# Stage 1 of a fused attention and expert kernel: score matmuls placed one by one, and the mixed tile moved to the front of its pair, with three products

## The chip, the cores and the metric

The kernel runs on one core of a Trainium2 chip. The time is that of one execution on the device in microseconds (us). Beside the runs that give the time, one execution is recorded by the hardware profiler, and all rows below are of that one.

## The reference

Three layers follow one another. The first is attention with pooled queries, the second a mixture of four small attention experts of which each token uses two, the third a gated layer with a causal convolution over five tokens. The change is in the first, which in the reference is:

```python
# q, k, v: 4 batches x 8 heads x 1152 x 64, float32
q_pool = q.reshape(B, H, S // 2, 2, D).mean(axis=3)          # 576 queries of a head
scores = scale * np.matmul(q_pool, k.transpose(0, 1, 3, 2))   # 576 x 1152
scores = scores - np.max(scores, axis=-1, keepdims=True)
attn = np.exp(scores)
attn = attn / (np.sum(attn, axis=-1, keepdims=True) + 1e-09)
out = np.matmul(attn, v)
```

## The kernel before

Stage 1 is this attention. It works through 16 pairs of heads, one after the other. A head has 576 queries, four blocks of 128 and a rest of 64, so a pair has nine score tiles of 128 queries by 1152 keys: four of each head, and one that holds the last 64 queries of both heads (called the mixed tile below). A tile goes through these steps:

- `scores` (L405): the tile's 1152 columns in three groups of 384, each in a PSUM bank of its own. Two score tiles fit in PSUM (pool `ps_s`, six banks).
- `rowmin` (L418, L421): VectorE reduces the tile to a row minimum `nm`. The scores carry a minus sign, so this is the maximum.
- `expo` (L423, L427): ScalarE takes the exponential from PSUM into `p` in SBUF and adds up the row.
- `transp` (L456, L464): TensorE transposes `p` in nine 128x128 pieces, three to a PSUM bank. One such three is called a T group here. Two banks serve all T groups (pool `ps_t`, tile `t`), and ScalarE (L472) or VectorE (L474) copies each group out into `pt`. The string table `EVAC` says which engine takes which group: one string for a tile of the pair, one letter for a group, D for VectorE and A for ScalarE.
- `av` (L476, L494), called a burst here: once per half of a pair (a unit), 18 matmuls multiply the transposed weights with the values. Before them the row sums' reciprocals are spread by transposes (L453), and after them VectorE multiplies the result by these (L496, `xf`). The burst's result lies in a bank of `ps_t` too.

Scores are made with split numbers. A float32 operand is cut into a high and a low part, each in the type `fp32r`. For a head's own tiles the 128 contraction rows hold the 64 dimensions twice: the high part of the queries above the low part (`qst`), against the same part of the keys in both halves (`ka` and `kb`, one for each head). Two matmuls, one for the keys' high part and one for the low, so give all four products. In the mixed tile the queries of head 0 stand beside zeros, and those of head 1 too, so that the two heads' results land on different rows; that takes two matmuls for each head, four for a group of columns.

The split itself is made for the next pair while one is worked on (`prep`, L359): GpSimd writes the high and low parts of queries and keys into `hlq` and `hlk`, and SyncE's DMAs copy them into `qst`, `ka` and `kb` (L377, L381 to L383).

The order of all this is written out by hand. `ORDER` (L399) is a string that is run through once per pair. S puts a group's score matmuls next (two, or four for the mixed tile), T a T group, X an exponential, H the reciprocals of a unit's sums, A a burst. The row minimum follows a tile's last S by itself (`score`, L621). `head` is called at the first S of each tile and carries GpSimd's and SyncE's work along. `UNITS` (L401) lists a pair's tiles: four in the first unit, and five in the second, of which the mixed tile (2, 4) is last. In pairs 1 to 9 VectorE also turns the third layer's weights into float32 during each burst (`decode`, L86 to L105).

TensorE takes its instructions in the order in which they were written, and so do the others. The engines wait for one another by semaphores.

Of the kernel before, what the change touches and what calls it, by code (L numbers as in the profile page):

```python
# [20 lines left out]
def tile_kernel(ctx, tc, q, k, v, w_gate, wq, wk, wv, wo, w_val, conv_w, w_out, wo_t, out):  # L21
    nc = tc.nc
# [294 lines left out]
    with ExitStack() as s1:  # L317
# [13 lines left out]
        for par in range(2):  # L331
            pair = [qpool.tile([P, 4 * P + 2 * R64], F32R, name=f"qst{par}{h}") for h in range(2)]
            act.activation(pair[0][:, 4 * P + R64:], zero, AF.Copy)
            act.activation(pair[1][:, 4 * P:4 * P + R64], zero, AF.Copy)
            qst.append(pair)
# [23 lines left out]
        def prep(n):  # L359
# [6 lines left out]
            data[n] = [qst[n % 2], kst, vn]  # L366
# [12 lines left out]
            def qmove():  # L379
                for r in range(2):  # L380
                    nc.sync.dma_start(f(qa[64 * r:64 * r + 64, 0:SQ]), f(hlq[0:64, r, :]))  # L381
                    nc.sync.dma_start(f(qb[64 * r:64 * r + 64, 0:512]), f(hlq[64:128, r, 0:512]))
                    nc.sync.dma_start(f(qb[64 * r:64 * r + 64, 512 + R64:]), f(hlq[64:128, r, 512:]))  # L383

            def qgroup():
                pool.tensor_scalar(qp, qp, -scale / 2, None, op0=ALU.mult)
                pool.tensor_copy(hlq[:, 0], qp)
                late.append(lambda: pool.tensor_tensor(out=hlq[:, 1], in0=qp, in1=f(hlq[:, 0]), op=ALU.subtract))
                late.append(qmove)
# [9 lines left out]
        ORDER = "TSTSSTTXSTTSSHTTXSTTSSTTXSSSASTSSTXSTTSSTTXSTTSSHTTXSTTSSTTSTXSSA"  # L399
        EVAC = ('DDA', 'ADD', 'AAD', 'DAA', 'DAD', 'DAA', 'DDA', 'ADD', 'AAA')  # L400
        UNITS = ([(0, 0), (0, 1), (1, 0), (1, 1)], [(0, 2), (0, 3), (1, 2), (1, 3), (2, 4)])  # L401
        tiles = [(n, u, i, ht) for n in range(len(pairs)) for u in range(2) for i, ht in enumerate(UNITS[u])]
        soft, pts, rss = {}, {}, {}

        def scores(m, g):  # L405
            n, u, i, (h, t) = tiles[m]
            qs, ks, vn = data[n]
            if g == 0:
                soft[m] = dict(s=ps_s.tile([P, G, 512], F32, name="s"))
            ps = soft[m]["s"][:, g, :]  # L410
            if h < 2:
                ops = [(qs[h][:, t * P:(t + 1) * P], ks[h][:, s, g * GW:(g + 1) * GW]) for s in range(2)]
# [10 lines left out]
        def expo(m):  # L423
            d = soft[m]
            n, u, i, _ = tiles[m]
# [3 lines left out]
        def shares(m):  # L429
# [3 lines left out]
            if i == k - 1:  # L433
# [6 lines left out]
                def copies():  # L440
                    eng = pool if n or u else dve
                    eng.tensor_copy(rm[:, 0:2].rearrange("p t (h d) -> p t h d", d=D), both)  # L442
                    if u == 1:
                        pool.tensor_copy(rm[:, 2], rs[:, 4:5].to_broadcast([P, P]))
# [3 lines left out]
        def spread_shares(n, u):  # L448
# [3 lines left out]
            for t in range(2 + u):  # L452
# [3 lines left out]
        def transp(m, g):  # L456
            n, u, i, (h, t) = tiles[m]
            p = soft[m]["p"]
            if i == 0 and g == 0:
                pts[n, u] = pt_p.tile([P, C, 2, 256 + R64 * u], F32, name=f"pt{u}")  # L460
# [15 lines left out]
        def av(n, u, between):  # L476
# [4 lines left out]
            N = 256 + R64 * u  # L481
# [5 lines left out]
            if u:  # L487
# [10 lines left out]
            def low():  # L498
                pool.tensor_tensor(out=xt[:, 1, :], in0=x, in1=f(xt[:, 0, :]), op=ALU.subtract)
                late.append(lambda: nc.sync.dma_start(f(x_d[b][:, hp, :, 256 * u:256 * u + N]), f(xt)))  # L500
# [9 lines left out]
        def first():  # L510

            b, hp = pairs[0]
            bufs = pt_p.tile([P, C, 2, 256 + R64], F32, name="pt1").rearrange("p c h q -> p (c h q)")
# [4 lines left out]
            data[0] = [qst[0], kst, vn]  # L518
# [10 lines left out]

            def qhigh(h, i):  # L530
                a, z = cuts[i]
                pool.tensor_scalar(qst[0][h][:, a + (R64 if h and i == 2 else 0):z + (R64 if h and i == 2 else 0)], qd[h][:, 0, a:z], -scale / 2, None, op0=ALU.mult)

            def qpart(h, i):
                a, z = cuts[i]
                o = R64 if h and i == 2 else 0
                qp = qd[h][:, 0]
                if i == 0:
                    act.activation(qst[0][h][:, a + o:z + o], qp[:, a:z], AF.Copy, scale=-scale / 2)
# [595 lines left out]
```

## Time and profile before

| what | value |
|---|---|
| time, median of three runs | 780.28 us (778.89 to 780.52) |
| the profiled execution's own time | 779.28 us |
| its span, first to last instruction | 777.5 us |
| TensorE busy | 756.8 us, 97% of the span |
| VectorE, ScalarE, GpSimd busy | 571.9, 447.9 and 306.5 us |
| stage 1, up to the last burst's start | 502.60 us |

The span is the stretch from the first instruction to the last. The profiled execution took 1.8 us more than its span, and 1.0 us less than the median. A matmul's recorded duration includes its way through the array, so that durations of neighbours overlap; what a matmul costs in a row of others is read from the distance between starts. A row with "x6" merges six neighbours of one kind: its first number is the start of the first one.

### The profile page before, as it was taken

What the parts mean: (1) busy time and instruction counts of PE and PEld (TensorE: products, weight loads), DVE (VectorE), ACT (ScalarE), POOL (GpSimd) and SP (SyncE); (2) the same over time, 40 slices, a digit from 0 to 9 for tenths busy, and PEclk for the clock granted to TensorE, in tenths of its full rate; (3) what the DMA queues carried; (4) which work ended last, traced back from release to release, by engine and by line L of the source; (5) the groups of instructions that cost most, each with busy time, mean ns of one, the idle gap of its engine ahead of it and who ended that gap; (6) DMA issues with size and microseconds to landing.
All of it is one profiled execution on the core that took longest, in us unless ns stands there. A gap on an engine that the chain in (4) does not pass through costs nothing.

```text
span 777.5 us, 14803 instructions
## 1 busy us (share of the span) xinstructions
PE 756.8 (97%) x5332; PEld 621.9 (80%) x5332; DVE 571.9 (74%) x1063; ACT 447.9 (58%) x988; POOL 306.5 (39%) x412
## 2 busy tenths in 40 slices
PE   6999999999999999999999999999999999989998
PEld 4777878778778778778787787888989889868887
DVE  5777888888988888756766675447679798888730
ACT  5566566466556656665664665425564554648632
POOL 4564574764765754743534511023222222220000
PEclk9999999999999999999999999999999999999999
DMA  7777867878789689668458483375545563900212
GB/s 237 184 194 222 246 180 232 230 202 248 186 240 265 171 242 266 158 199 244 111 171 230 123 258 123 90 205 112 167 108 123 134 186 93 293 1 14 81 57 94
DMA packets 86825, 134.51 MB, mean 173 GB/s; under 512 B 21600, under 2 KB 58976, under 8 KB 86752
## 3 DMA queue, kind: packets, MB, share of 16 engines
q1 hardware_dynamic: 86752, 133.57, 61.2%
q8 instruction: 42, 0.69, 0.4%
q14 instruction: 31, 0.25, 0.1%
HBM read 53.37 MB, written 21.76 MB: 97 GB/s over the span
## 4 chain that ended last, share of the span: by engine, by line
PE 86%; DVE 7%; ACT 3%; issue 1%; SPq 1%; DMA 1%; POOL 1%; POOLq 0%; DVEq 0%; ACTq 0%
PE s L416 21%; PE t L464 20%; PE t L494 18%; PE a L242 7%; PE o L1051 6%; PE a L275 4%; PE a L850 3%; PE s L750 2%; PE a L715 2%; DVE gp L215 2%; PE a L822 1%; PE t L453 1%; SPq L524 1%; ACT p L771 1%; DVE nm L760 1%
## 5 line engine op out<-in xcount | busy, mean ns | idle before, releaser
L421 DVE TENSOR_REDUCE nm<-s 128x1 f32<-128x1152 f32 x144 | 195.4, 1357 | 37.3 <-PE s L416 30.9
L427 ACT ACTIVATE p<-s,nm 128x1152 f32<-128x1152 f32 x144 | 175.9, 1222 | 37.0 <-DVE nm L421 28.3
L464 PE MATMUL t<-ident,p 128*128 128x128 f32 x1296 | 194.2, 280 | 2.5 <-DVE pt L474 1.9
L472 ACT ACTIVATE pt<-t 128x384 f32<-128x384 f32 x224 | 99.9, 489 | 146.1 <-PE t L464 136.7
L464 PEld LDWEIGHTS t<-ident,p 128*128 128x128 f32 x1296 | 147.0, 141 | 41.4 <-ACT pt L472 17.1
L494 PE MATMUL t<-pt,vn 128*64 128x320 f32 (+1 forms) x1152 | 146.8, 408 | 0.0
L416 PE MATMUL s<-ka,qst 128*128 128x384 f32 x480 | 127.9, 370 | 6.8 <-ACT ka L545 6.8
L494 PEld LDWEIGHTS t<-pt,vn 128*64 128x64 f32 x1152 | 80.0, 137 | 55.8 <-issue 5.3
L416 PE MATMUL s<-kb,qst 128*128 128x384 f32 x480 | 120.8, 360 | 1.0 <-ACT p L427 0.9
L474 DVE COPY pt<-t 128x384 f32<-128x384 f32 x208 | 107.3, 548 | 13.1 <-PE t L464 10.0
L416 PEld LDWEIGHTS s<-kb,qst 128*128 128x128 f32 x480 | 79.7, 191 | 8.3 <-issue 6.2
L416 PEld LDWEIGHTS s<-ka,qst 128*128 128x128 f32 x480 | 78.2, 193 | 8.2 <-ACT ka L545 7.2
L786 POOL TENSOR_TENSOR p<-p,sm 128x512 f32<-128x512 f32 (+3 forms) x32 | 40.1, 1253 | 110.2 <-DVE sm L784 81.9
L442 POOL COPY rm<-rs 128x256 f32<-128x256 f32 x31 | 12.4, 400 | 130.4 <-DVE rs L437 122.5
L496 DVE TENSOR_TENSOR xf<-t,rb 128x256 f32<-128x256 f32 (+1 forms) x32 | 14.7, 458 | 63.2 <-PE t L494 62.3
L771 ACT ACTIVATE p<-s,nm 128x256 f32<-128x256 f32 (+3 forms) x64 | 33.1, 524 | 22.7 <-DVE nm L760 22.6
L371 POOL TENSOR_TENSOR hlk<-kt,hlk 128x384 fp32r<-128x384 f32 x45 | 45.2, 1005 | 1.0
L242 PE MATMUL a<-xh,wqk 128*128 128x288 f32 x288 | 43.0, 299 | 2.1 <-DVE pt L800 2.1
L215 DVE SCALAR_TENSOR_TENSOR gp<-x,cw,gp 128x572 f32<-128x572 f32 (+3 forms) x48 | 40.7, 849 | 2.6 <-ACT gp L871 2.1
L503 POOL CAST xt<-xf 128x256 fp32r<-128x256 f32 (+1 forms) x32 | 13.6, 424 | 72.6 <-DVE xf L496 72.5
L242 PEld LDWEIGHTS a<-xh,wqk 128*128 128x128 f32 x288 | 39.4, 188 | 3.1 <-DVE pt L800 2.5
L760 DVE TENSOR_REDUCE nm<-s 128x2 f32<-128x512 f32 (+4 forms) x40 | 32.4, 811 | 1.4
(176 smaller groups left out, 1091.9 us busy)
## 6 DMA issues: line engine op xcount, KB each, us to landing
ka<-hlk SPq DMA_DIRECT2D x90, 192.0 KB, 3.2
kb<-hlk SPq DMA_DIRECT2D x90, 192.0 KB, 3.6
vn<-in_v_dram SPq DMA_DIRECT2D x16, 576.0 KB, 7.8
k<-hl SPq DMA_DIRECT2D x32, 288.0 KB, 4.9
qt<-in_q_dram SPq DMA_DIRECT2D x15, 576.0 KB, 5.3
kt<-in_k_dram SPq DMA_DIRECT2D x15, 576.0 KB, 6.3
xh<-x_d SPq DMA_DIRECT2D x12, 576.0 KB, 6.2
x_d<-xt SPq DMA_DIRECT2D x16, 320.0 KB, 4.0
```

What stands on the lines that cost most here:

```text
L215: dve.scalar_tensor_tensor(out=gp[:, n:], in0=x[:, 0:SQ - n], scalar=cw[:, m, c:c + 1], in1=gp[:, n:], op0=ALU.mult, op1=ALU.add)
L242: pe.matmul(ps[:, 0:HQ], lhsT=wqk[wi][:, t, cs], rhs=xh[t][xi][:, qsl], start=o == 0, stop=o == len(ops) - 1)
L371: late.append(lambda: pool.tensor_tensor(out=hlk[:, 1, gs], in0=kt[:, gs], in1=f(hlk[:, 0, gs]), op=ALU.subtract))
L416: pe.matmul(ps[:, 0:GW], lhsT=a, rhs=c, start=o == 0, stop=o == len(ops) - 1)
L421: dve.tensor_reduce(d["nm"], d["s"][:, :, 0:GW], axis=AX.XY, op=ALU.min)
L427: act.activation(d["p"], d["s"][:, :, 0:GW], AF.Exp, bias=d["nm"], scale=-1.0, accum_out=sums[(2 * n + u) % len(sums)][:, i:i + 1])
L464: pe.transpose(ps[:, j * P:(j + 1) * P], p[:, g, j * P:(j + 1) * P], ident)
L472: act.activation(dst, src, AF.Copy)
L474: dve.tensor_copy(dst, src)
L494: pe.matmul(ps[64 * h:64 * h + 64, 0:N], lhsT=vn[:, h, j, :], rhs=pt[:, j, h, :], start=j == 0, stop=j == C - 1)
L771: act.activation(p[:, e * w:(e + 1) * w], ps[:, e, 0:w], AF.Exp, bias=nm[:, e:e + 1], scale=-1.0, accum_out=sm[:, e:e + 1])
L1051: pe.matmul(ps[:, 0:w], lhsT=hl[xi][:, kt, t * P - a:(t + 1) * P - a], rhs=end3["wo3"][:, kt, wi, c:c + w], start=o == 0, stop=o == len(op ...
```

## The change

The score matmuls are placed one by one. An S of the new `ORDER` is one matmul for a tile of a head, so that a T group can stand between the two matmuls of a group of columns. The row minimum gets a letter of its own, R, and the string is written anew.

The mixed tile becomes the first of its pair and of the first unit, which so has five tiles and the second four. The queries are reordered on the way in, so that the mixed tile holds queries 256 to 319. Its products are made in another way, except in pair 0: the operand `mixed` has the high and the low part of both heads' 64 queries as blocks on a diagonal, with zeros beside them, and it is multiplied with `hlk`, the split keys of both heads as GpSimd wrote them. High by high, low by high and high by low are three matmuls, in place of four; the product of the two low parts is not made. `mixed` is written by GpSimd in two copies. `qst` is 64 columns shorter, and two DMAs of a pair fall away. `EVAC` is written anew as well, with 13 D and 14 A as before.

```diff
-            data[n] = [qst[n % 2], kst, vn]
+            data[n] = [qst[n % 2], kst, vn, hlk]
...
-                    nc.sync.dma_start(f(qa[64 * r:64 * r + 64, 0:SQ]), f(hlq[0:64, r, :]))
-                    nc.sync.dma_start(f(qb[64 * r:64 * r + 64, 0:512]), f(hlq[64:128, r, 0:512]))
-                    nc.sync.dma_start(f(qb[64 * r:64 * r + 64, 512 + R64:]), f(hlq[64:128, r, 512:]))
+                    nc.sync.dma_start(f(qa[64 * r:64 * r + 64]), f(hlq[0:64, r, 0:4 * P]))
+                    nc.sync.dma_start(f(qb[64 * r:64 * r + 64]), f(hlq[64:128, r, 0:4 * P]))
+
+            def qlow():
+                pool.tensor_tensor(out=hlq[:, 1], in0=qp, in1=f(hlq[:, 0]), op=ALU.subtract)
+                for h in range(2):
+                    hs = slice(64 * h, 64 * h + 64)
+                    pool.tensor_copy(mixed[hs, :, hs], f(hlq[hs, :, 4 * P:]))
...
-        EVAC = ('DDA', 'ADD', 'AAD', 'DAA', 'DAD', 'DAA', 'DDA', 'ADD', 'AAA')
-        UNITS = ([(0, 0), (0, 1), (1, 0), (1, 1)], [(0, 2), (0, 3), (1, 2), (1, 3), (2, 4)])
+        EVAC = ('AAA', 'DDA', 'ADD', 'AAD', 'DAA', 'DDA', 'AAD', 'AAD', 'DDD')
+        UNITS = ([(2, 4), (0, 0), (0, 1), (1, 0), (1, 1)], [(0, 2), (0, 3), (1, 2), (1, 3)])
+        FIRST = ([(0, 0), (0, 1), (1, 0), (1, 1), (2, 4)], UNITS[1])
...
-                ops = [(qs[hh][:, 4 * P:], ks[hh][:, s, g * GW:(g + 1) * GW]) for hh in range(2) for s in range(2)]
-            for o, (a, c) in enumerate(ops):
-                pe.matmul(ps[:, 0:GW], lhsT=a, rhs=c, start=o == 0, stop=o == len(ops) - 1)
+                ops = [(last0[hh], ks[hh][:, s, gs]) for hh in range(2) for s in range(2)]
+            per = max(1, len(ops) // slots(m))
+            for c in range(o * per, min(len(ops), (o + 1) * per)):
+                pe.matmul(ps[:, 0:GW], lhsT=ops[c][0], rhs=ops[c][1], start=c == 0, stop=c == len(ops) - 1)
...
+            elif n:
+                ops = [(mixed[:, wi], kboth[:, xi, gs]) for wi, xi in THREE]
...
+                elif c == "R":
+                    if nr < M:
+                        rowmin(nr)
+                    nr += 1
```

The following rows show TensorE's program in the first unit of the second pair before the change: scores of one head's tiles (L416, `s<-ka` and `s<-kb`), T groups (L464, three transposes each), the spreading of the sums (L453), and the burst (L494).

```order
L464 MATMUL t<-ident,p 128x128 x6
L416 MATMUL s<-ka,qst_138 128x384 x2
L464 MATMUL t<-ident,p 128x128 x6
L416 MATMUL s<-ka,qst_138 128x384 x4
L464 MATMUL t<-ident,p 128x128 x6
L416 MATMUL s<-ka,qst_138 128x384 x2
L464 MATMUL t<-ident,p 128x128 x6
L416 MATMUL s<-ka,qst_138 128x384 x4
L464 MATMUL t<-ident,p 128x128 x6
L416 MATMUL s<-kb,qst_139 128x384 x6
L453 MATMUL t<-ident,rm 128x128 x2
```

And these show it after the change, from the mixed tile's matmuls of one pair (L433, `s<-hlk,mixed`) to the next tile's; L482 are the T groups.

```order
L433 MATMUL s<-hlk,mixed 128x384
L482 MATMUL t<-ident,p 128x128 x6
L433 MATMUL s<-hlk,mixed 128x384 x5
L482 MATMUL t<-ident,p 128x128 x3
L433 MATMUL s<-hlk,mixed 128x384 x3
L482 MATMUL t<-ident,p 128x128 x6
L433 MATMUL s<-ka,qst_134 128x384 x2
L482 MATMUL t<-ident,p 128x128 x3
L433 MATMUL s<-ka,qst_134 128x384
L482 MATMUL t<-ident,p 128x128 x3
L433 MATMUL s<-ka,qst_134 128x384 x2
L482 MATMUL t<-ident,p 128x128 x3
```

Two T groups in a row were parted by two or four score matmuls by turns. Now two in a row have at least three matmuls ahead of them in nearly every place, and many T groups stand alone, with one or two matmuls between.

The next rows are VectorE's program around the burst of a pair's first unit (256 columns) in the stretch in which it decodes weights, before the change: copies of T groups (L474), two row minima (L421), the seven decoding steps (L105 to L102), the burst's product (L496), and what follows.

```order
L474 COPY pt_1010<-t 128x3x128 x2
L421 TENSOR_REDUCE nm<-s 128x1 x2
L105 SCALAR_TENSOR_TENSOR dec_1001<-dec_998,dec_1001 128x256
L92 TENSOR_SCALAR dec_1184<-wraw 128x256
L94 TENSOR_SCALAR dec_1185<-wraw 128x256
L96 SCALAR_TENSOR_TENSOR dec_1185<-wraw,dec_1185 128x256
L98 TENSOR_SCALAR dec_1187<-wraw 128x256
L100 TENSOR_SCALAR dec_1186<-dec_1185 128x256
L102 SCALAR_TENSOR_TENSOR dec_1187<-dec_1187,dec_1186 128x256
L496 TENSOR_TENSOR xf_1151<-t,rb 128x256
L474 COPY pt_1201<-t 128x3x128
L421 TENSOR_REDUCE nm<-s 128x1
```

And after the change, around the burst of a pair's second unit, which now has the 256 columns (L492 copies, L438 row minima, L514 the burst's product).

```order
L492 COPY pt_786<-t 128x3x128 x2
L438 TENSOR_REDUCE nm<-s 128x1 x2
L105 SCALAR_TENSOR_TENSOR cw<-dec_834,cw 128x20
L92 TENSOR_SCALAR dec_1003<-wraw 128x256
L94 TENSOR_SCALAR dec_1004<-wraw 128x256
L96 SCALAR_TENSOR_TENSOR dec_1004<-wraw,dec_1004 128x256
L98 TENSOR_SCALAR dec_1006<-wraw 128x256
L100 TENSOR_SCALAR dec_1005<-dec_1004 128x256
L102 SCALAR_TENSOR_TENSOR dec_1006<-dec_1006,dec_1005 128x256
L514 TENSOR_TENSOR xf_973<-t,rb 128x256
L438 TENSOR_REDUCE nm<-s 128x1
L492 COPY pt_1027<-t 128x3x128 x2
```

VectorE has the same kinds of work on both sides of the burst. Behind the product of this burst no copy comes first any more: the three copies of the mixed tile, whose T groups follow it, are ScalarE's. Ahead of the burst the two copies are the last two T groups of the unit, and both row minima stand behind them.

## Rows read from the trace of the kernel before

**Rows 1.** The page: busy time, then the chain that ended last.

```profile
PE 756.8 (97%) x5332; PEld 621.9 (80%) x5332; DVE 571.9 (74%) x1063; ACT 447.9 (58%) x988; POOL 306.5 (39%) x412
...
PE 86%; DVE 7%; ACT 3%; issue 1%; SPq 1%; DMA 1%; POOL 1%; POOLq 0%; DVEq 0%; ACTq 0%
PE s L416 21%; PE t L464 20%; PE t L494 18%; PE a L242 7%; PE o L1051 6%; PE a L275 4%; PE a L850 3%; PE s L750 2%; PE a L715 2%; DVE gp L215 2%; PE a L822 1%; PE t L453 1%; SPq L524 1%; ACT p L771 1%; DVE nm L760 1%
```

**Rows 2.** Windows: busy us of PE, PEld, DVE, ACT, POOL; clock; DMA.

```profile
160.00:200.00 40.00, 40.00 (x288) 30.40 (x287) 35.48 (x56) 25.06 (x50) 27.10 (x38) 1.00 0.74 203
...
440.00:480.00 40.00, 40.00 (x289) 31.80 (x286) 27.63 (x40) 23.97 (x46) 8.92 (x15) 1.00 0.67 215
```

**Rows 3.** Timeline of PE, one pair: start, us, line, names, count, idle.

```profile
103.77 5.07 PE L494 MATMUL t<-pt,vn 128*64 128x320 f32 x36
108.77 0.55 PE L464 MATMUL t<-ident,p 128*128 128x128 f32 x3
...
111.16 0.59 PE L416 MATMUL s<-ka,qst 128*128 128x384 f32 x2
111.65 0.93 PE L464 MATMUL t<-ident,p 128*128 128x128 f32 x6
112.34 0.96 PE L416 MATMUL s<-ka,qst 128*128 128x384 f32 x4
113.13 0.82 PE L464 MATMUL t<-ident,p 128*128 128x128 f32 x6
...
114.89 0.94 PE L416 MATMUL s<-ka,qst 128*128 128x384 f32 x4
...
116.24 1.29 PE L416 MATMUL s<-kb,qst 128*128 128x384 f32 x6
117.37 0.38 PE L453 MATMUL t<-ident,rm 128*128 128x128 f32 x2
117.68 4.11 PE L494 MATMUL t<-pt,vn 128*64 128x256 f32 x36
121.72 0.62 PE L416 MATMUL s<-kb,qst 128*128 128x384 f32 x2
122.18 0.49 PE L464 MATMUL t<-ident,p 128*128 128x128 f32 x3
...
132.52 0.55 PE L464 MATMUL t<-ident,p 128*128 128x128 f32 x3
```

**Rows 4.** The same timeline, twelve pairs later.

```profile
466.71 1.57 PE L494 MATMUL t<-pt,vn 128*64 128x320 f32 x10
```

**Rows 5.** Waits: engine and line, whom for, us in total, times, longest.

```profile
PEld t L464 <- ACT pt L472: 17.1, 76, 0.5
...
PEld t L464 <- DVE pt L474: 4.0, 10, 1.3
...
PEld t L464 <- DVE xf L496: 2.8, 15, 0.5
```

**Rows 6.** Timeline of ScalarE and GpSimd around one exponential.

```profile
100.31 1.23 ACT L427 ACTIVATE p<-s,nm 128x1152 f32<-128x1152 f32 x1 [0.25 <-DVE rs L436]
...
100.99 0.29 POOL L444 COPY rm<-rs 128x128 f32<-128x128 f32 x1
...
101.72 0.87 ACT L472 ACTIVATE pt<-t 128x384 f32<-128x384 f32 x2
```

**Rows 7.** The page, groups: engine, operation, count, busy us, mean ns.

```profile
L472 ACT ACTIVATE pt<-t 128x384 f32<-128x384 f32 x224 | 99.9, 489 | 146.1 <-PE t L464 136.7
...
L474 DVE COPY pt<-t 128x384 f32<-128x384 f32 x208 | 107.3, 548 | 13.1 <-PE t L464 10.0
```

**Rows 8.** Timeline of VectorE around a burst in the decoding stretch.

```profile
117.57 1.36 DVE L421 TENSOR_REDUCE nm<-s 128x1 f32<-128x1152 f32 x1 [0.35 <-PE s L416]
118.84 0.41 DVE L105 SCALAR_TENSOR_TENSOR dec<-dec,dec 128x256 f32<-128x256 int32 x1
...
121.91 0.42 DVE L496 TENSOR_TENSOR xf<-t,rb 128x256 f32<-128x256 f32 x1
```

More of the change, by code (lines that the diff above doesn't have):

```diff
@@ L331, in tile_kernel @@
         for par in range(2):
[L332 to L335, printed above, removed]
+            qst.append([qpool.tile([P, 4 * P], F32R, name=f"qst{par}{h}") for h in range(2)])
+        last0 = [qpool.tile([P, P], F32R, name=f"last{h}") for h in range(2)]
+        mixed = qpool.tile([P, 2, P], F32R, name="mixed")
+        for h in range(2):
+            act.activation(last0[h][:, 64 - 64 * h:128 - 64 * h], zero, AF.Copy)
+            for r in range(2):
+                act.activation(mixed[64 * h:64 * h + 64, r, 64 - 64 * h:128 - 64 * h], zero[64 * h:64 * h + 64], AF.Copy)
         sums = [sums_p.tile([P, 5], F32, name=f"sums{i}") for i in range(3)]
@@ L387, in qgroup @@
                 pool.tensor_copy(hlq[:, 0], qp)
-                late.append(lambda: pool.tensor_tensor(out=hlq[:, 1], in0=qp, in1=f(hlq[:, 0]), op=ALU.subtract))
+                late.append(qlow)
                 late.append(qmove)
@@ L451, in spread_shares @@
             ps = ps_t.tile([P, 512], F32, name="t")
-            for t in range(2 + u):
+            for t in range(3 - u):
                 pe.transpose(ps[:, t * P:(t + 1) * P], rm[:, t], ident)
@@ L459, in transp @@
             if i == 0 and g == 0:
-                pts[n, u] = pt_p.tile([P, C, 2, 256 + R64 * u], F32, name=f"pt{u}")
+                pts[n, u] = pt_p.tile([P, C, 2, 256 + R64 * (1 - u)], F32, name=f"pt{u}")
             pt = pts[n, u]
@@ L512, in first @@
             b, hp = pairs[0]
-            bufs = pt_p.tile([P, C, 2, 256 + R64], F32, name="pt1").rearrange("p c h q -> p (c h q)")
+            bufs = pt_p.tile([P, C, 2, 256], F32, name="pt1").rearrange("p c h q -> p (c h q)")
             bufs = [bufs[:, i * S:(i + 1) * S] for i in range(4)]
@@ L548, in first @@
             qadd(0, 0, dve)
-            for h, i in ((1, 0), (0, 1), (0, 2), (1, 1), (1, 2)):
+            for h, i in ((1, 0), (0, 2), (1, 2), (0, 1), (1, 1)):
                 qadd(h, i, pool)
@@ L596, in head @@
                     preps = prep(n + 1)
-                if (u, i) == (1, 1) and n + 2 < len(pairs):
+                if (u, i) == (1, 0) and n + 2 < len(pairs):
                     load(n + 2)
@@ L619, in filler, with score @@
                 late2.clear()
-        def score(k, g):
-            if g == 0:
+        seq = [(m, g, o) for m in range(M) for g in range(G) for o in range(slots(m))]
+        seq += [(M + i, g, o) for i in range(9) for g in range(G) for o in range(2)]
+        def score(k, g, o):
+            if g == o == 0:
                 head(k - 1)
             if k < M:
-                scores(k, g)
-                if g == 2:
-                    rowmin(k)
-            if g == 2:
+                scores(k, g, o)
+            if (g, o) == (2, 1):
                 if preps:
@@ L634, in between @@
             def between():
[L635 to L636 removed]
+                if nx < M:
+                    expo(nx)
                 for _ in range(9):
@@ L651, in tile_kernel @@
             for g in range(G):
-                scores(m, g)
+                for o in range(slots(m)):
+                    scores(m, g, o)
             rowmin(m)
@@ L655, in tile_kernel @@
                 preps.pop(0)()
-        ns, nx = 9, 2
+        ns, nr, nx = 21, 3, 2
+        ends = [9 * n + i for n in range(len(pairs)) for i in (4, 8)]
+        spread, bursts = iter(ends), iter(ends)
         for n in range(len(pairs)):
@@ L659, in tile_kernel @@
                 if c == "S":
-                    score(ns // 3, ns % 3)
+                    score(*seq[ns])
                     ns += 1
+                elif c == "R":
+                    if nr < M:
+                        rowmin(nr)
+                    nr += 1
                 elif c == "T":
@@ L677, in tile_kernel @@
                 elif c == "H":
-                    shares(9 * n + (3 if nt < 27 * n + 12 else 8))
+                    shares(next(spread))
                 elif c == "A":
-                    burst(nt // 3 - 1)
+                    burst(next(bursts))
                     nx += 1
```

47 lines of the change are left out of this document (26 added, 21 removed).

## The prediction

> **What bounds the kernel now.** I read the page's busy line and chain first. TensorE is busy for 97% of the span, and 86% of the chain that ended last is its own work, most of it in stage 1's three lines: scores, transposes and bursts [rows 1]. Then I took the windows, to see that this holds all through stage 1 and at which clock: TensorE is busy for 40.00 us of 40, at a granted clock of 1.00, with VectorE at 35.48 us while it decodes weights and at 27.63 us later [rows 2]. A busy TensorE may still lose time, so the timeline came third. From one burst to the same burst twelve pairs later, 103.77 to 466.71 us, is 362.94 us, or 30.25 us for a pair [rows 3, 4].
>
> How much of 30.25 us is work? Six score matmuls take 1.29 us where four take 0.94 us, so one is 0.175 us. A T group is (0.82 - 0.49) = 0.33 us, from six and three transposes. A burst to the next instruction is 5.00 us (103.77 to 108.77) or 4.04 us (117.68 to 121.72), and the spread transposes before it take 0.31 us (117.37 to 117.68) for two and, at 0.11 us for one more, 0.42 us for three [rows 3]. A pair has 60 score matmuls (10.5 us), 27 T groups (8.9 us), the bursts (9.04 us) and the spreads (0.73 us): 29.2 us. So about 1.05 us of a pair is waiting inside busy time.
>
> Where that is, the same rows show. The two matmuls at 111.16 us are followed by transposes 0.49 us later, where four take 0.79 us (112.34 to 113.13) and two should so take 0.44 us; and six transposes take 0.93 us at 111.65 us but 0.82 us at 113.13 us [rows 3]. A late pair of T groups costs 0.05 + 0.11 = 0.16 us. Single groups show it too, at 0.55 us in place of 0.49 us; in this pair seven runs of transposes are late, the first at 108.77 us and the last at 132.52 us. Seven times 0.16 us is 1.1 us, which is the gap. The waits name the cause: the weight loads of the transposes wait for the copies of earlier groups, 76 + 10 times, and 15 times for a burst's product, about six a pair [rows 5]. Two banks serve all T groups, and behind only two score matmuls the bank is not yet empty.
>
> **The change part by part.** *Three products for four.* Three matmuls go in each of pairs 1 to 15, pair 0 keeping its four: 45 x 0.175 = 7.9 us, on the engine that is the chain. Operand types and shapes stay, so I price the new ones like the old.
>
> The Trainium skill has another price for this: "TensorE: Matmul & The Clock Gate", section "Back-to-back issue gap", gives columns / 2.4 + 2.5 ns, an estimate of 0.1625 us for 384 columns and of 7.3 us for the 45. The trace shows 0.175 us, and the sum goes by that.
>
> *The new order.* A pair's work becomes 29.2 - 0.53 = 28.7 us. What waits remain I worked out by laying the rows' durations end to end in the new order by hand, for one pair. A row minimum takes 1.36 us [rows 8]; an exponential holds ScalarE for 1.41 us (100.31 to 101.72) [rows 6]; a lone copy takes 0.49 us on ScalarE and 0.55 us on VectorE [rows 7]. A bank is then free about 1.1 us after its group began. Most places now give it that: three matmuls (0.53 us) and one or two T groups lie between a group and its bank's next use. Five are late. The second group of the pair's third tile waits some 0.17 us and the first group of the sixth tile some 0.24 us, both for ScalarE copies that stand behind an exponential. Three others are late by 0.02 to 0.05 us. That is 0.5 us, and each late group adds its reload, half of the 0.11 us above: 0.3 us more. I take 0.8 us against 1.05 us. Below, the bound is no wait at all; above, every run is late (a rival).
>
> In pairs 1 to 9 VectorE's backlog at the second unit's burst counts too. By the hand layout both row minima stand behind two copies and end 2.2 us after the burst's start, where before the last one ended 1.25 us after it (117.57 + 1.36 against 117.68) [rows 3, 8]. Decoding then takes 3.0 us (118.93 to 121.91) and the product 0.42 us, so it ends 5.6 us after the start of a burst of 4.04 us, 1.6 us after the burst. It holds a bank that the next pair's second T group wants six matmuls and one T group after the burst, at 1.38 us: 0.2 us late, in eight or nine pairs. That makes 0.9 us for these and 0.8 us for the others.
>
> So a pair takes 28.7 + 0.85 = 29.5 us, 0.75 us less than 30.25. Times 15 this is 11.3 us, of which 7.9 us are the matmuls and 3.4 us the waits.
>
> The Trainium skill speaks of the boundary between scores and transposes: the same page, "Step-by-step: what each phase is for", says that the next weights are loaded while a matmul runs. By that rule alone a T group behind a score matmul costs nothing extra however often the two alternate, which gives the second rival below. The trace bears it out where the bank is free (113.13 us) and not where the load itself waits for the bank (111.65 us) [rows 3].
>
> *GpSimd and DMAs.* Two copies into `mixed` are added per pair. The nearest row copies 128 columns in 0.29 us [rows 6], so at most 0.6 us. They are behind the split of the queries, nearly a whole pair ahead of their use, on an engine that is busy for 27 of 40 us at most [rows 2]; behind them only key splits wait, which have 10 us or so. Cost zero; without that cover 0.6 us a pair. Keys for the mixed tile no longer pass through a DMA, so nothing there gets later. `hlk` may be written again only when the mixed tile's nine matmuls are done, and these are done before the next keys are split; what queues behind that write on GpSimd is the spread of sums, which has some 0.7 us left before its burst. The two DMA issues that fall away are on a queue that TensorE does not wait for: zero.
>
> *Start and end.* Pair 0 has its twelve mixed matmuls earlier, and in the last pair four gate projections move ahead of the last burst, so that the next stage's scores follow it directly and could wait for the burst's product, at 0.6 us after it (121.72 to 121.91 + 0.42) [rows 3, 8]. The last pair also has fewer T groups in a row without scores between. I take +1 us gained for both ends, with -1 and +2 as bounds.
>
> Sum: 779.28 - 11.3 - 1.0 = 767.0 us against the profiled execution. The median was 1.0 us above that one, within the spread of the three runs, so I leave 767.0.
>
> **The rivals.** *Only the matmuls go.* If ScalarE's exponentials make as many groups late as before, 1.05 us of waiting stay: 779.3 - 7.9 = 771.4. For it speaks that ScalarE's copies are already the ones waited for 76 times of 101 [rows 5], against it that the groups in question had two matmuls ahead of them and now have three. *All waits go.* 28.7 us a pair, 1.55 x 15 = 23 us, 756. The hand layout is tight in five places by a few hundredths, and a small slip either way decides them. *Every run of transposes is late.* The new order has 20 runs of T groups in a pair, where it had 16. At 0.16 us each 20 late runs cost 3.2 us, a pair takes 31.9 us, and the kernel 24 us more: 803. It turns slower than before at 1.58 us of waits, which is ten late runs of 20; at thirteen, the likelier case of this kind, 30.8 us a pair and 787. Seven late runs of 16 before speak for its possibility; that the late ones were those behind two matmuls speaks against it. *VectorE becomes the bound while it decodes.* It has 35.48 / 40 x 30.25 = 26.8 us of work in such a pair [rows 2], 91% of 29.5 us. If its queue so holds up the row minima that these nine pairs gain nothing, six pairs gain 0.75 us and the ends 1 us: 5.5 us, 774.
>
> **How the numbers follow.** About 0.2%, 1.6 us, is what can be told from no change. My forecast, 763 to 770, gets 0.50; only the matmuls, or VectorE's bound, 770 to 777, 0.22; waits all gone, 755 to 763, 0.16; within 0.2% of before, where start and end eat what the pairs gain, 0.05; transposes late, slower, 0.07. Faster is 0.50 + 0.22 + 0.16 = 0.88. For 8 in 10 the range leaves out the slower cases, no change and the outer ends: 756 to 775.
>
> **What would show it.** The period between bursts should be near 29.5 us in the middle pairs, and a little longer in pairs 2 to 9. Score matmuls should number 915 in place of 960, at the same distance of 0.175 us. Loads of transposes waiting for copies should still appear, four to six a pair. The product of the second unit's burst should run a microsecond or more after the burst in the decoding pairs. The prediction is wrong if the period is over 30 us, if matmuls from `mixed` take more than 0.2 us, or if more than half of the runs of transposes wait.

## The result, and the profile after

The changed kernel takes 772.76 us (median of four runs, 771.62 to 774.07), beside 779.59 us of the kernel before on the same chip (four runs, 778.84 to 780.52): a ratio of 0.9912, 95% interval 0.9889 to 0.9936. That is 6.8 us faster, where 12.3 us had been forecast; 772.76 us lies inside the range of 756 to 775 us. The profiled execution took 771.89 us, with a span of 770.1 us in place of 777.5 us, so the traces have 7.4 us to account for. Among the experiments below, one execution took 1053.1 us at a mean granted clock of 0.66 and is left out of that experiment's numbers.

The page after the change: TensorE's busy time with the other engines', then the chain that ended last, by engine and by line.

```profile
PE 746.0 (97%) x5287; PEld 614.9 (80%) x5287; DVE 568.8 (74%) x1064; ACT 449.1 (58%) x990; POOL 314.3 (41%) x441
...
PE 87%; DVE 6%; DMA 2%; ACT 2%; issue 1%; SPq 1%; POOL 0%; POOLq 0%; DVEq 0%; ACTq 0%
PE s L433 22%; PE t L482 19%; PE t L512 18%; PE o L1079 7%; PE a L242 6%; PE a L275 4%; PE a L878 3%; PE s L778 2%; PE a L743 2%; PE a L850 2%; DVE gp L215 1%; PE t L471 1%; DMA xh<-x_d 1%; DMA y<-wot_d 1%; PE a L734 1%
```

TensorE has 5332 - 5287 = 45 matmuls fewer, is still the chain, and its three largest lines have nearly the same shares as before [rows 1]. Two entries of the chain's last line are new DMAs that TensorE waits for: `y<-wot_d`, 3.0 us in all, and `xh<-x_d`, 0.3 us.

TensorE's timeline from the second unit's burst of the third pair (256 columns now) to the same burst twelve pairs later, with the places in between that the prediction spoke of; columns are start, duration, line and names.

```profile
103.07 4.11 PE L512 MATMUL t<-pt,vn 128*64 128x256 f32 x36
107.10 0.80 PE L433 MATMUL s<-kb,qst 128*128 128x384 f32 x3
...
108.65 0.88 PE L482 MATMUL t<-ident,p 128*128 128x128 f32 x6
109.29 0.77 PE L433 MATMUL s<-kb,qst 128*128 128x384 f32 x3
109.89 0.82 PE L482 MATMUL t<-ident,p 128*128 128x128 f32 x6
...
111.08 0.97 PE L482 MATMUL t<-ident,p 128*128 128x128 f32 x6
...
114.67 0.55 PE L482 MATMUL t<-ident,p 128*128 128x128 f32 x3
...
117.11 0.49 PE L482 MATMUL t<-ident,p 128*128 128x128 f32 x3
...
126.13 1.13 PE L433 MATMUL s<-hlk,mixed 128*128 128x384 f32 x5
127.09 0.49 PE L482 MATMUL t<-ident,p 128*128 128x128 f32 x3
...
129.03 0.55 PE L482 MATMUL t<-ident,p 128*128 128x128 f32 x3
...
309.63 4.11 PE L512 MATMUL t<-pt,vn 128*64 128x256 f32 x36
...
456.20 4.11 PE L512 MATMUL t<-pt,vn 128*64 128x256 f32 x36
```

From 103.07 to 456.20 us are 353.13 us, 29.43 us a pair, where it was 30.25 us [rows 3, 4]: 9.81 us gained in twelve pairs, 0.82 us each. The first seven of them, in which VectorE decodes, take 29.51 us each (103.07 to 309.63), the last five 29.31 us. The five mixed matmuls and the way to the next group take 0.96 us (126.13 to 127.09), and of a head's, three take 0.60 us with that way (109.29 to 109.89) and two more 0.35 us at the price of the prediction, 0.95 us: the new operands cost no more. Four runs of transposes are plainly late, at 108.65 us (0.88 us for six in place of 0.82), 111.08 us (0.97), 114.67 and 129.03 us (0.55 in place of 0.49); the one at 117.11 us is not.

The waits of the transposes' weight loads: line, whom for, us in total, times, longest.

```profile
PEld t L482 <- ACT pt L490: 6.8, 31, 0.5
...
PEld t L482 <- DVE pt L492: 2.3, 15, 0.2
PEld t L482 <- DVE xf L514: 2.1, 7, 0.7
```

These are 53 waits of 11.2 us, where there were 101 of 23.9 us [rows 5]. ScalarE's copies held up the loads 76 times, and do so 31 times now, twice a pair.

VectorE at the burst of 103.07 us, in the stretch in which it decodes weights:

```profile
102.38 2.61 DVE L438 TENSOR_REDUCE nm<-s 128x1 f32<-128x1152 f32 x2
...
108.18 0.42 DVE L514 TENSOR_TENSOR xf<-t,rb 128x256 f32<-128x256 f32 x1
...
110.42 1.02 DVE L492 COPY pt<-t 128x384 f32<-128x384 f32 x2 [0.27 <-PE t L482]
```

Two row minima now stand in this burst, and its product starts 1.1 us after the burst's end (107.10 to 108.18 us), as the hand layout had it; before it was 0.2 us [rows 3, 8]. The bank that it holds is the one that the run of 108.65 us is late for. The run of 111.08 us is late for the second of the two copies at 110.42 us. VectorE had been idle for 0.27 us before the first, until the transposes were there, so the second stands behind the first and not behind a row minimum.

Now the end of stage 1. TensorE after the change, from the last burst; a number in brackets is idle time and what ended it.

```profile
489.62 6.03 PE L275 MATMUL a<-wvg,xh 128*128 128x260 f32 x48
...
495.80 4.11 PE L512 MATMUL t<-pt,vn 128*64 128x256 f32 x36
500.53 0.74 PE L778 MATMUL s<-k,q 128*128 128x256 f32 x4 [0.62 <-DVE xf L514]
...
511.89 0.94 PE L734 MATMUL a<-y,y 128*128 128x512 f32 x3 [2.65 <-DMA y<-wot_d]
513.16 4.07 PE L734 MATMUL a<-y,y 128*128 128x512 f32 x9 [0.34 <-DMA y<-wot_d]
517.07 0.60 PE L850 MATMUL a<-ident,p 128*128 128x128 f32 x4
```

The same stretch of the kernel before:

```profile
507.59 6.07 PE L275 MATMUL a<-wvg,xh 128*128 128x260 f32 x48
513.49 0.66 PE L750 MATMUL s<-k,q 128*128 128x256 f32 x4
...
521.96 2.91 PE L706 MATMUL a<-y,y 128*128 128x512 f32 x12
524.71 0.60 PE L822 MATMUL a<-ident,p 128*128 128x128 f32 x4
```

The four gate projections (L275) stood behind the last burst and stand ahead of it now. The folding of the output weights (L706, now L734) waits 2.65 and 0.34 us for `wot_d`, and its remaining nine matmuls, from 513.16 us to the next line at 517.07 us, take 3.91 us, where all twelve took 2.75 us. The windows show why (busy us of PE, PEld, DVE, ACT, POOL; then clock, DMA share, GB/s):

```profile
512.00:513.00 1.00, 0.82 (x3) 0.34 (x3) 0.00 (x0) 0.00 (x0) 0.01 (x1) 1.00 1.15 278
...
515.00:517.00 2.00, 2.00 (x6) 1.43 (x5) 0.00 (x0) 0.00 (x0) 0.00 (x0) 0.54 1.05 222
517.00:520.00 3.00, 3.00 (x20) 2.68 (x19) 0.34 (x3) 2.21 (x6) 0.00 (x0) 1.00 0.98 207
```

The first three matmuls behind the wait still have a granted clock of 1.00 (2.4 GHz; 512 to 513 us). It falls while the nine that follow run: 0.54 from 515 to 517 us, 1.2 GHz for nearly all of it, and 1.00 again from 517 us on. The Trainium skill ("TensorE: Matmul & The Clock Gate", "HAM oscillation — how this bites in real kernels") describes that a wait for data between bursts of matmuls lets the clock fall, and that the next burst starts at the low clock. The trace agrees that the clock falls behind such a wait, with 3.91 us for nine, but here the first matmuls behind it run at the full clock, and the clock falls only in the run of nine.

SyncE issues, after the change and then before, show how late the weights are (start and duration of the issue):

```profile
501.88 0.36 SPq L518 DMA_DIRECT2D x_d<-xt  x1
...
505.20 3.27 SPq L726 DMA_DIRECT2D y<-wot_d  x4
```

```profile
...
513.13 2.04 SPq L698 DMA_DIRECT2D y<-wot_d  x4
```

The weights were issued 8.8 us before TensorE wanted them (513.13 to 521.96), and the want now comes 4.0 us after the issue (505.20 to 511.89 - 2.65). They stand behind the last write of `x_d`, which needs the last burst, and the gates that used to cover that way are gone.

The ledger: at the third pair's burst the change is 0.70 us ahead (103.77 to 103.07); the twelve pairs give 9.81; from there to the next stage's first scores 2.45 more (46.78 us to 513.49, now 44.33 us to 500.53); from these scores to L850 5.32 are lost (11.22 and 16.54 us); the rest of the program takes 0.24 us longer. Sum 7.4 us. At these bursts the changed kernel has its pair's wide burst behind it, since the first unit is now the wide one, and the kernel before has it still to do, 0.96 us more (5.07 for 4.11). With that counted in, the start gives 0.70 + 0.96 - 2 x 0.82 = 0.0 us, and the last pair 2.45 - 0.96 - 0.82 = 0.7 us beyond its own gain.

### The profile page after: what moved, and what is told of

Same layout as the page of the kernel before. It is cut to its first block, busy times and chain, and to the rows that moved or that the text cites. A ratio compares the mean times of both kernels' runs of the same rounds, so it can differ in the third digit from the quotient of the medians.

```text
span 770.1 us, 14724 instructions
## 1 busy us (share of the span) xinstructions
PE 746.0 (97%) x5287; PEld 614.9 (80%) x5287; DVE 568.8 (74%) x1064; ACT 449.1 (58%) x990; POOL 314.3 (41%) x441
## 4 chain that ended last, share of the span: by engine, by line
PE 87%; DVE 6%; DMA 2%; ACT 2%; issue 1%; SPq 1%; POOL 0%; POOLq 0%; DVEq 0%; ACTq 0%
PE s L433 22%; PE t L482 19%; PE t L512 18%; PE o L1079 7%; PE a L242 6%; PE a L275 4%; PE a L878 3%; PE s L778 2%; PE a L743 2%; PE a L850 2%; DVE gp L215 1%; PE t L471 1%; DMA xh<-x_d 1%; DMA y<-wot_d 1%; PE a L734 1%
## 5 line engine op out<-in xcount | busy, mean ns | idle before, releaser
L438 DVE TENSOR_REDUCE nm<-s 128x1 f32<-128x1152 f32 x144 | 192.2, 1353 | 15.4 <-PE s L433 15.2
L482 PE MATMUL t<-ident,p 128*128 128x128 f32 x1296 | 199.7, 276 | 0.6 <-DVE xf L514 0.3
L482 PEld LDWEIGHTS t<-ident,p 128*128 128x128 f32 x1296 | 150.1, 141 | 26.1 <-ACT pt L490 6.8
L512 PE MATMUL t<-pt,vn 128*64 128x256 f32 (+1 forms) x1152 | 146.7, 408 | 0.0
L492 DVE COPY pt<-t 128x384 f32<-128x384 f32 x208 | 110.4, 555 | 46.8 <-PE t L482 43.0
L512 PEld LDWEIGHTS t<-pt,vn 128*64 128x64 f32 x1152 | 80.0, 137 | 55.9 <-issue 5.3
L433 PE MATMUL s<-ka,qst 128*128 128x384 f32 x384 | 116.6, 386 | 6.6 <-ACT ka L565 6.6
L433 PE MATMUL s<-kb,qst 128*128 128x384 f32 x384 | 100.7, 371 | 1.5 <-ACT p L445 0.9
L433 PEld LDWEIGHTS s<-kb,qst 128*128 128x128 f32 x384 | 61.3, 191 | 16.4 <-issue 13.2
L433 PEld LDWEIGHTS s<-ka,qst 128*128 128x128 f32 x384 | 64.5, 194 | 7.9 <-ACT ka L565 7.0
L514 DVE TENSOR_TENSOR xf<-t,rb 128x320 f32<-128x320 f32 (+1 forms) x32 | 14.6, 457 | 49.5 <-PE t L512 48.5
L521 POOL CAST xt<-xf 128x320 fp32r<-128x320 f32 (+1 forms) x32 | 13.7, 428 | 70.1 <-DVE xf L514 69.4
L433 PE MATMUL s<-hlk,mixed 128*128 128x384 f32 x135 | 33.7, 357 | 0.0
```

The costliest lines, as they stand in the source:

```text
L433: pe.matmul(ps[:, 0:GW], lhsT=ops[c][0], rhs=ops[c][1], start=c == 0, stop=c == len(ops) - 1)
L438: dve.tensor_reduce(d["nm"], d["s"][:, :, 0:GW], axis=AX.XY, op=ALU.min)
L482: pe.transpose(ps[:, j * P:(j + 1) * P], p[:, g, j * P:(j + 1) * P], ident)
L492: dve.tensor_copy(dst, src)
L512: pe.matmul(ps[64 * h:64 * h + 64, 0:N], lhsT=vn[:, h, j, :], rhs=pt[:, j, h, :], start=j == 0, stop=j == C - 1)
```

## The experiments

The theory to be tested: TensorE's pairs gain as forecast, some 0.53 us by the matmuls left out and 0.3 us by the order with its copies, and the entry into the next stage gives 5.3 us back, because the gate projections no longer stand behind the last burst. Against it stand that the late weights only show a loss that the DMA engines would bring anyway, that the matmuls were hidden and the order gained it all, or that the start costs a microsecond.

**Gate projections behind the last burst.** The changed kernel, with the last four fillers, the gate projections, held back until the order is through:

```diff
-            if m >= M + 2:
+            if m >= M + 2 and ended:
...
-            if fill:
+            if fill and more:
...
-                        filler()
+                        filler(len(fill) > 4)
...
+        ended.append(1)
```

> The changed kernel, but the four gate projections of stage 2's first batch stand behind the last burst of stage 1 again, as before the change. Theory A (the entry to stage 2 lost its cover: the folding matmuls wait for weights whose load is queued behind the last burst's result, and the clock drops in that wait): the 5.2 us of matmuls that run after the burst let the loads land, the waits of the folding matmuls for the DMA go, TensorE's clock stays at 1.00 there, and the time falls by 4 to 5.5 us, to about 768. Theory B (the loads are late because of stage 2's own DMA traffic, whatever stands before them): the waits stay and the time is within 1 us of the changed kernel, 772 to 774.

Measured: 767.42 us (766.59 to 768.92), ratio to before 0.9847 (0.9832 to 0.9863), 5.3 us below the changed kernel's, and 4.7 us below by the spans (765.4 and 770.1 us). TensorE around the last burst:

```profile
491.15 4.11 PE L512 MATMUL t<-pt,vn 128*64 128x256 f32 x36 [0.53 <-ACT rb L504]
495.19 6.06 PE L275 MATMUL a<-wvg,xh 128*128 128x260 f32 x48
501.08 0.66 PE L781 MATMUL s<-k,q 128*128 128x256 f32 x4
...
509.54 2.91 PE L737 MATMUL a<-y,y 128*128 128x512 f32 x12
512.30 0.60 PE L853 MATMUL a<-ident,p 128*128 128x128 f32 x4
```

The folding runs through in 2.91 us, and its clock is 1.00. L853 starts at 512.30 us in place of 517.07 us, 11.22 us after the next stage's first scores, as in the kernel before. The place of these 48 matmuls alone is the loss at the entry.

**Weights issued first.** The changed kernel, gates still ahead of the burst; only the four loads of `wot_d` go ahead of the loads of `x_d` on SyncE:

```diff
...
+    for t in range(KT):
+        nc.sync.dma_start(f(wot[:, t]), f(wot_d[:, t]))
     parts += [load_part(1, x2b_p.tile([P, SQ], F32, name="x2"), 2 + k) for k in range(2)]
...
-    for t in range(KT):
-        nc.sync.dma_start(f(wot[:, t]), f(wot_d[:, t]))
```

> The changed kernel with the loads of the folding weights (wot) issued ahead of the six loads of batch 1's input; the gate projections stay ahead of the last burst. Theory A (the folding matmuls are late because their loads are queued last behind the burst's result): the loads are issued near 502 us in place of 505, the 5.2 us of the first twelve folding matmuls shrink to about 2.8 and their 2.65 us of waiting ahead go, so 3 to 5 us faster, 768 to 770, unless batch 1's projections now wait for their input, which are needed some 8 us later. Theory B (the loads are slow because 16 DMA queues are full at that time, at a share of 1.0): the folding matmuls still wait for 2 us or more, and the time stays at 771 to 773.

Measured: 773.78 us (770.17 to 774.73), ratio 0.9915 (0.9896 to 0.9934): nothing gained. Two of the six runs took 770.17 and 771.22 us at a mean granted clock of 0.998; the other four, at 0.995, took 773.55 us and more. TensorE at the folding and 14 us later, then the windows there:

```profile
509.53 2.91 PE L734 MATMUL a<-y,y 128*128 128x512 f32 x12
...
523.72 1.19 PE L778 MATMUL s<-k,q 128*128 128x256 f32 x4 [4.92 <-DMA q<-hl]
```

```profile
515.00:520.00 5.00, 3.80 (x26) 3.07 (x24) 4.00 (x12) 2.30 (x5) 1.62 (x2) 1.00 1.01 211
...
525.00:530.00 5.00, 5.00 (x24) 4.95 (x24) 2.13 (x4) 1.52 (x6) 0.00 (x0) 0.52 0.00 0
```

The folding is on time, so its own wait was the weights' place in the queue. But the keys and queries that follow in that queue are late in its place: TensorE waits 4.92 us for `q<-hl`, and the clock is 0.52 behind it. The DMA engines are fully busy meanwhile (share 1.01 from 515 to 520 us), so the order of the queue chose only who waits. What helped, in the run before this one, was work for TensorE in that time.

**Four products again.** The changed kernel with low by low as a fourth matmul for each group of the mixed tile's columns:

```diff
-                ops = [(mixed[:, wi], kboth[:, xi, gs]) for wi, xi in THREE]
+                ops = [(mixed[:, wi], kboth[:, xi, gs]) for wi, xi in THREE + ((1, 1),)]
...
```

> The changed kernel with the fourth product (low part of the queries by low part of the keys) put back into the mixed tile of pairs 1 to 15, as a matmul right behind the third: 45 matmuls more, the new order otherwise. Theory A (TensorE is the bound, a matmul costs its distance of 0.175 us): 7.9 us slower than the changed kernel, about 780.5, and a pair of 29.9 us. That would leave the new order by itself with a gain of some 0.3 us a pair, 4 to 5 us, eaten by start and entry. Theory B (the waits for PSUM banks take up what is removed): 2 to 5 us slower, 775 to 778.

Measured: 778.85 us (777.99 to 780.76), ratio 0.9992 (0.9981 to 1.0002). The bursts of the third and the fifteenth pair, the folding of the weights, and a window there:

```profile
105.23 4.11 PE L512 MATMUL t<-pt,vn 128*64 128x256 f32 x36
...
464.57 4.11 PE L512 MATMUL t<-pt,vn 128*64 128x256 f32 x36
...
520.00 2.35 PE L734 MATMUL a<-y,y 128*128 128x512 f32 x9 [2.35 <-DMA y<-wot_d]
...
523.58 0.60 PE L850 MATMUL a<-ident,p 128*128 128x128 f32 x4
```

```profile
520.00:525.00 5.00, 4.57 (x24) 3.53 (x25) 0.05 (x1) 1.14 (x3) 0.39 (x1) 1.00 1.06 264
```

359.34 us are 29.95 us a pair: three matmuls cost 0.52 us, as priced, and the order alone is worth 30.25 - 29.95 = 0.30 us a pair. The order so gains 4.5 us in 15 pairs. This kernel is 4.6 us ahead of the kernel before at the next stage's first scores (508.92 and 513.49 us) and 1.1 us ahead at L850 (523.58 and 524.71 us), so it loses 3.4 us at the entry, where the changed kernel loses 5.3.

The difference is the clock. The folding waits here too, for 2.35 us and then for 0.43 us more, but the clock stays at 1.00. From its first matmul to L850 it takes 3.58 us, 0.43 us of it waiting; in the changed kernel that is 5.18 us (511.89 to 517.07), 0.34 us of it waiting. So about 1.7 us of the loss of 5.3 us is the lower clock, and the rest is there without it. This is most of why the whole kernel is only 6.1 us slower than the changed one, and not 7.8.

**Three products in the kernel before.** No new order, no new tile: one of the mixed tile's four matmuls is left out, so head 1's queries there are not multiplied with the low part of its keys.

```diff
-                ops = [(qs[hh][:, 4 * P:], ks[hh][:, s, g * GW:(g + 1) * GW]) for hh in range(2) for s in range(2)]
+                ops = [(qs[hh][:, 4 * P:], ks[hh][:, s, g * GW:(g + 1) * GW]) for hh in range(2) for s in range(2)][:4 if n == 0 else 3]
```

> The kernel before the change with one of the mixed tile's four matmuls left out in pairs 1 to 15 (the low part of head 1's keys is not multiplied for the last 64 queries), order and all else as before. Theory A (TensorE's own matmuls are the bound in the old order too): 7.9 us faster than before, about 771.5 to 772, a pair of 29.7 us. Theory B (in the old order the freed time turns into waits for the two banks, since the mixed tile's four matmuls stood between transposes): 3 to 6 us faster, a pair of 29.9 to 30.1 us.

Measured: 772.90 us (median of five runs, 772.62 to 774.78), ratio 0.9921 (0.9907 to 0.9935), the same as the whole change.

```profile
102.40 5.07 PE L494 MATMUL t<-pt,vn 128*64 128x320 f32 x36
...
458.77 5.07 PE L494 MATMUL t<-pt,vn 128*64 128x320 f32 x36
```

29.70 us a pair, 0.55 us less than before, with the transposes' waits for ScalarE as they were (17.2 us, 77 times). Matmuls and order add up: 0.55 + 0.30 is 0.85 us, and the change gained 0.82. At the end of stage 1 this kernel is 8.5 us ahead (the last burst at 494.08 us in place of 502.60); it keeps 6.4 of the span. The rest goes where the second batch's inputs are loaded:

```profile
619.42 1.01 PE L242 MATMUL a<-xh,wqk 128*128 128x288 f32 x3 [0.50 <-DMA xh<-x_d]
```

There TensorE waits 0.50 us for a DMA, with another 1.06 us for VectorE shortly before, and the clock from 617 to 622 us is 0.75 as a mean; before the change it waited for VectorE alone there, at a clock of 1.00.

**The old copies.** The changed order with the table of copies of before, moved along with the tiles:

```diff
-        EVAC = ('AAA', 'DDA', 'ADD', 'AAD', 'DAA', 'DDA', 'AAD', 'AAD', 'DDD')
+        EVAC = ('AAA', 'DDA', 'ADD', 'AAD', 'DAA', 'DAD', 'DAA', 'DDA', 'ADD')
```

> The changed kernel with the table of copies from before the change, its strings moved along with their tiles (mixed tile AAA, then DDA ADD AAD DAA DAD DAA DDA ADD); four of the nine strings differ from the changed kernel's. Theory A (the waits of transposes are for banks whose copy stands behind an exponential or a row minimum, so which engine copies decides them): more waits of transpose weight loads for copies than the 46 of the changed kernel, a pair of 29.7 to 30.1 us, the kernel 4 to 10 us slower. Theory B (the number of matmuls ahead of a transpose alone decides): pair and time within 1 us of the changed kernel.

Measured: 795.78 us (794.89 to 796.62), ratio 1.0209 (1.0194 to 1.0224). The waits of its transposes:

```profile
PEld t L482 <- DVE pt L492: 23.5, 46, 0.7
...
PEld t L482 <- ACT pt L490: 12.8, 32, 0.8
```

From 108.20 us to 479.91 us it takes 30.98 us a pair, 1.55 us more than the changed kernel, several times what was expected. The direction was right and the size was not. Loads of transposes wait 78 times, five a pair, 36.3 us in all, and TensorE stands still at these transposes 45 times, for 17.7 us. The work on TensorE is the same. Which engine empties which bank is worth 23 us here, three times the 45 matmuls.

**The start.** Pair 0's first tile copied by VectorE in place of ScalarE, so that the third exponential comes sooner:

```diff
-            if EVAC[m % 9][g] == "A":
+            if ("DDA" if m == 0 else EVAC[m % 9])[g] == "A":
```

> The changed kernel with one string of the table of copies changed for the very first tile of pair 0: its first two copies on VectorE and the third on ScalarE (DDA), in place of all three on ScalarE (AAA). Theory A (the start of stage 1 loses 1.1 us because the third tile's exponential, at 18.73 us, stands behind two copies on ScalarE, and the fifth tile's scores wait for it until 20.08 us): the exponential starts near 17 us, the first pair's second burst starts 0.8 to 1.5 us earlier, at 43.0 to 43.7 us in place of 44.48, and the time falls by about 1 us, to 771.7. Theory B (the start loses it to the stretch at half clock from 15.10 to 18.51 us): the burst stays at 44.2 to 45 us unless that stretch happens not to come in this run.

Measured: 771.88 us (770.80 to 772.67), ratio 0.9901 (0.9886 to 0.9916). That exponential starts at 16.86 us in place of 18.73 us and TensorE's wait of 1.29 us for it (at 20.08 us) is gone, but VectorE is late with other work instead, and pair 0's second burst comes only 0.15 us sooner (44.33 and 44.48 us). By the times alone, 0.9 us less with ranges that overlap, this is no clear gain. The stretch at half clock, 0.51 from 15.0 to 18.5 us in the changed kernel, doesn't come here either (1.00), and the burst is hardly sooner for that, so neither theory is borne out. It agrees with the ledger, where the start is worth nothing.

**Both repairs.** Gates behind the burst, and this start.

> Both mends together: the four gate projections behind the last burst, and DDA for the first tile of pair 0. If they add up, 5.3 us from the entry to stage 2 and 1 us from the start, about 766.3, 14 us faster than the kernel before the change. If the start is set by the clock and not by the copies, 767.4 as with the first mend alone.

Measured: 766.47 us (766.02 to 767.30), ratio 0.9833 (0.9819 to 0.9847). It was run again beside the next experiment:

> The version with both edits (gate projections behind the last burst, pair 0's first tile copied by VectorE) once more on the same chip as the one above, to be compared with it: 766.5 by either theory, as it was (766.0 to 767.3).

Measured: 767.18 us (766.37 to 768.59), ratio 0.9832 (0.9814 to 0.9851). This version is 13 us faster than before, and faster than the changed kernel by 6 us. From the gates alone (767.42 us, 766.59 to 768.92) it can't be told apart by the times.

**One copy moved.** The late run of 111.08 us waits for the second of two copies on VectorE. On top of both repairs, the first copy of that tile goes to ScalarE, which is idle for 0.25 us just then:

```diff
-        EVAC = ('AAA', 'DDA', 'ADD', 'AAD', 'DAA', 'DDA', 'AAD', 'AAD', 'DDD')
+        EVAC = ('AAA', 'ADA', 'ADD', 'AAD', 'DAA', 'DDA', 'AAD', 'AAD', 'DDD')
```

> On top of the version with the gate projections behind the last burst and pair 0's first tile copied by VectorE: in the table of copies the pair's second tile becomes ADA in place of DDA, so the first copy of that tile goes from VectorE to ScalarE, in every pair. In the changed kernel the third run of transposes of a pair (405.46 us, 0.97 us for six) waits 0.155 us because its bank is emptied by VectorE's second copy (404.81 us, 1.02 us for two), which stands behind a row minimum; ScalarE is idle for 0.26 us just then. Theory A (late banks are what a pair still loses, and this one is VectorE's): the run takes 0.82 us, ScalarE's next copies come some 0.2 us later and the next group is late by up to 0.2 us in place of it where that shows; between 0 and 0.15 us a pair, 0 to 2.3 us gained, I take 1 us: about 765.5. Rival B (ScalarE has no room: its exponentials and all copies behind them slide): the period grows by 0.1 to 0.3 us, 768 to 771.

Measured: 772.26 us (770.52 to 773.58), ratio 0.9894 (0.9874 to 0.9914), 5.1 us slower than the version it is built on. TensorE at that run, one pair:

```profile
410.29 0.84 PE L482 MATMUL t<-ident,p 128*128 128x128 f32 x6
411.38 0.62 PE L433 MATMUL s<-ka,qst 128*128 128x384 f32 x2 [0.26 <-ACT p L445]
```

The run is no longer late (0.84 us), as the theory had it. But the way from it to the next scores is 1.09 us in place of 0.73 us: the exponential behind the moved copy starts 0.43 us later (3.57 us after the burst's end, and 3.14 us without the edit), and it is what empties the bank of the scores. The rival was right, and short in size: 29.69 us a pair is 0.38 us more than without the edit (29.31 us), where 0.1 to 0.3 had been expected.

## Why the prediction was right or wrong

The sign was right, and so was what the pairs gain; the forecast missed one loss, at the end of stage 1, of about the size by which it is off.

*Three products for four.* Forecast 7.9 us; 0.52 us a pair in one experiment and 0.55 us in the other, 7.8 to 8.3 us. Right: TensorE is the chain here, so work left out was time gained, and the row gave its price. Over the whole kernel 6.1 and 6.4 us of it are seen, since waits and clock elsewhere differ between the runs compared. The Trainium skill's formula ("TensorE: Matmul & The Clock Gate", "Back-to-back issue gap"), which the page gives for a single matmul by itself, gave an estimate of 7.3 us, and the runs side with the row.

*The new order.* Forecast 3.4 us of waits; measured 0.30 us a pair, 4.5 us. By the prediction's own durations a pair is 28.7 us of work, so 0.7 us of waits are left where 0.8 to 0.9 us were expected. Of the places named, the two largest were not the right ones: the second group of the third tile (112.23 us) and the first of the sixth (117.11 us) are on time, with 0.49 us each, and the run at 111.08 us waits for VectorE's second copy, not for a copy of ScalarE's behind an exponential. The layout by hand gave the number of late runs (four or so a pair), not which, so that its sum came out is in part luck. Waits of loads for copies are 46, three a pair, where four to six had been expected. The product of the second unit's burst was foreseen: it does come 1.1 us after the burst, the run at 108.65 us is late for its bank, and the decoding pairs take 0.2 us more than the later ones (29.51 and 29.31 us), where 0.1 us had been forecast. Before the change that difference was 0.1 us (30.28 and 30.19 us).

*GpSimd and DMAs.* Forecast zero. No run parts them from the order: the 0.30 us a pair contains what they cost. In the list of the changed kernel's waits no line of stage 1 on TensorE (L433, L471, L482, L512) waits for GpSimd or a DMA.

*Start and end.* This is the step that failed: "I take +1 us gained for both ends, with -1 and +2 as bounds." The start gave 0.0 us and the last pair 0.7 us, as far as right; but the entry into the next stage lost 5.3 us. The step saw the gate projections move ahead of the last burst, and looked only for the next reader of that burst, at 0.6 us (0.62 us measured). It did not follow the burst's result further, to the write of `x_d` and through SyncE's queue to the loads behind it. The numbers for it were in the trace of before. The loads of `wot_d` were issued 8.8 us before their use, 5.9 us of that were the gates (507.59 to 513.49 us), and this row of the DMAs there has the time from issue to landing last:

```profile
y<-wot_d SPq DMA_DIRECT2D x4, 256.0 KB, 6.6
```

8.8 - 5.9 leaves 2.9 us for a transfer of 6.6 us: an estimate of 3.7 us of waiting, which would have made the forecast 771 us before any loss of clock. Measured were 2.99 us of waits and, by the comparison with four products, some 1.7 us of lower clock.

*The rivals.* "Only the matmuls go", 771.4 us, is the nearest number, and it is not what happened: the waits did go, by 0.3 us a pair. "Every run of transposes is late" did not come about here, but the old table of copies costs about what was priced for thirteen late runs (30.98 us a pair, and 30.8), by fewer and longer waits. (For all twenty late the prediction has 24 us; its own numbers give 24.8.) VectorE is not the bound in the decoding pairs: they take 29.51 us, so they gain 0.77 us. Nor did all waits go, since some 0.7 us a pair is left.

What stays open is which of the copies in the old table cause its 1.55 us a pair: waits for both engines grow, and no run moved them one by one. It is open too why the clock fell behind a wait of 2.65 us and not behind one of 2.35 us.

## What to carry to other kernels

When an order moves work ahead of an event, list everything that the event starts, the transfers above all, and ask what TensorE does until the last of them lands; work that seems to be idle filler may be the cover of a whole queue. With two alternating banks, the table of which engine empties them belongs to the order: whether an engine can take one more copy is not read from its idle time, but from the slack of what stands behind that copy. And take the price of a removed matmul from rows, since on the bounding engine of these pairs it came back in full.

## What the runs showed of the hardware

A wait of TensorE of 2.65 us cost more than its length: the granted clock was 0.54 in the two microseconds that followed 515 us, and nine matmuls took 3.91 us, where twelve take 2.75 us at 1.00. In the kernel with the weights first the wait was 4.92 us, and the clock 0.52 from 525 to 530 us. It isn't so each time: with four products a wait of 2.35 us left the clock at 1.00.

Where the scores' banks are all in use, 0.43 us of delay in one exponential was 0.36 us of TensorE, in every pair (0.73 to 1.09 us). The Trainium skill ("Perfetto Trace Analysis", "Matmuls") advises to rotate groups of matmuls through banks so that the emptying lies beside the next group. The trace shows how little room that leaves once every bank is taken.
